# A convolution's setup rearranged: rounding of the angle tables moved from DVE to Pool, x loads between the tables, h copied in four parts, x's first stage woven into h's spectra

## Chip, cores, metric

One core of one Trainium2 chip. The metric is the device time of one execution in microseconds (us), median of the runs; lower is better. DVE is VectorE, ACT ScalarE, POOL GpSimd, PE TensorE, PEld its weight loads, SP SyncE. To evict is to copy a matmul's result out of the accumulators (PSUM) into SBUF. "Third stage" below is the first matmul of the convolution's third stage, the landmark by which the setup is measured: everything before it is setup, everything behind it the change doesn't touch.

## The reference

```python
Xf = np.fft.rfft(x, n=2*S, axis=1)            # x (8, 5696, 128), h (5696, 128)
Hf = np.fft.rfft(h, n=2*S, axis=0)
y  = np.fft.irfft(Xf * Hf[None], n=2*S, axis=1)[:, :S]
theta = y @ w_theta
yr = einsum('ts,bsd->btd', w_tok_r, y*cos(theta)); yi = einsum('ts,bsd->btd', w_tok_i, y*sin(theta))
u = y + yr + yi
out = u + maximum(u @ w_ch, 0)
```

## The kernel before

The convolution runs as four stages of matmuls with tables of sines: f1 (first stage), w (twiddles, second stage), r (third), e (fourth). The tables are computed on the chip: Pool makes angles, DVE reduces them to a fraction of a turn, ACT takes the sine. (Adding the constant MAGIC and taking it off again rounds to a whole number; a cosine needs the absolute value as well.) The spectra of h (its second-stage results) are made once and kept in memory; then come eight groups of x, and behind them the large matmuls that take most of the time. The order in which instructions stand in each engine's queue is made when the kernel is built, from the order in the code and estimated readiness; each engine then works its queue strictly in order.

```python
def turns_of(pattern, base, lanes, m, per, quarter=None):     # angle -> turns in [-0.5, 0.5]
    t, k = (two tiles of 11*NB floats, two buffers each)
    nc.gpsimd.iota(k, pattern=pattern, base=base, ...)
    nc.gpsimd.tensor_scalar(t, k, lanes, 1.0 / per, op0=mult, op1=mult)
    if quarter is not None: quarter(t)
    nc.vector.tensor_scalar(k, t, MAGIC, None, op0=add)                            # rounding
    nc.vector.scalar_tensor_tensor(t, k, MAGIC, t, op0=ALU.subtract, op1=ALU.subtract)
    return t, k

def absolute(k, r):
    nc.vector.scalar_tensor_tensor(k, r, -1.0, r, op0=mult, op1=ALU.max)

def w_table(k0):                                              # 15 of 90 columns: 960 elements
    t, k = turns_of([[1, 15], [N1, N2]], k0, lane[:, 0:1], P, NF)
    sine(w_t2[:, k0:k0 + 15, :N2], t3, 1)
    cosine(w_t2[:, k0:k0 + 15, N2:2 * N2], t3, k3)            # absolute, then ACT
    nc.vector.tensor_scalar(w_t2[..., 2 * N2:], w_t2[..., :N2], -1.0, None, op0=mult)

for k0 in (0, 15, 30):
    w_table(k0)
nc.vector.tensor_copy(h16[:NB], u_t[...])                     # h, one copy
x16s = {0: load_x(0)}                                         # 16 transfers of x
steps, a_h = stage_a(h16, True)                               # first stage of h, DVE and ACT evict
woven(steps, [w_table(45), w_table(60), w_table(75)])
for c in range(NCK):
    h_chunk(c)                                                # spectra of h
...
a0, load0, b0 = front(0)                                      # first stage of x, ACT alone evicts
woven(a0, [r_table(0, r_u), r_table(1, r_v), s_table] + load0)
woven(b0, [e_table(n0) for n0 in range(0, EN, 11)])           # second stage and products
```

## Time and profile before

| | before |
|---|---|
| median of 3 runs | 2176.91 us (2175.84 to 2178.12) |
| span of the profiled run | 2175.5 us |
| copy of h starts | 12.5 us |
| x's first stage is over (its second begins) | 63.6 us |
| third stage | 86.6 us |
| DVE busy up to it, idle | 67.3 us, 19.3 us |

The stretches, the timeline of the start and the groups that carry this are shown in the prediction. To read them: busy times of one engine may be added up, those of several may not, since engines work beside each other; an idle stretch of an engine counts only where that engine sets the end.

### The profile page before, as it was taken

Reading aid. Unit: us, or ns where it says so; the run is one execution under the profiler, and the core shown is the slowest. Engines: PE = TensorE matmul, PEld = TensorE weight load, DVE = VectorE, ACT = ScalarE, POOL = GpSimd, SP = SyncE. Lnnn points to the kernel's source line nnn. Section 1 sums busy time; section 2 is a strip of 40 time slices with the busy share of each in tenths; the row PEclk is TensorE's granted clock in tenths of the full one; section 3 lists DMA queues with packets and bytes.
Section 4 is the critical chain, followed back from the end, with each engine's and each line's share of the span. In section 5 each row is a group of like instructions: output and inputs, shape, how many; then the busy total and the mean of one; then the engine's idle time right before and its main releaser. Section 6 shows DMA issues by size and latency. Waiting matters only on the chain.

```text
span 2175.5 us, 41105 instructions
## 1 busy us (share of the span) xinstructions
PE 1998.2 (92%) x15545; PEld 1125.1 (52%) x15723; DVE 1619.4 (74%) x2920; ACT 670.6 (31%) x984; POOL 857.1 (39%) x1572
## 2 busy tenths in 40 slices
PE   4788898763899999999999999899999999999998
PEld 4787888652344444444444444344444444444444
DVE  7767767767778888888877667667777777776867
ACT  5877877574132333333210000001111111111111
POOL 5301010002344645445466544354545453535350
PEclk8788889987899999999999999999999999999999
DMA  7356463579988989899999869687878787879794
GB/s 146 89 125 163 128 162 118 172 185 275 236 156 175 182 169 168 167 179 176 176 169 162 138 115 291 106 133 137 148 132 152 132 151 130 152 131 153 126 158 91
DMA packets 409382, 340.38 MB, mean 156 GB/s; under 512 B 83303, under 2 KB 363751, under 8 KB 408071
## 3 DMA queue, kind: packets, MB, share of 16 engines
q0 software_dynamic: 221312, 143.00, 48.7%
q1 hardware_dynamic: 183552, 179.93, 28.5%
q10 hardware_dynamic: 4320, 14.81, 1.8%
q8 instruction: 123, 2.02, 0.4%
q14 instruction: 75, 0.61, 0.1%
HBM read 381.83 MB, written 97.93 MB: 221 GB/s over the span
## 4 chain that ended last, share of the span: by engine, by line
PE 65%; DMA 5%; DVE 4%; issue 2%; ACT 2%; POOL 1%; SPq 1%; DVEq 0%; ACTq 0%; POOLq 0%
PE m L910 59%; DMA b<-z_hbm 3%; PE m L878 2%; DMA z_hbm<-zz 2%; DVE c L917 1%; PE v L680 1%; PE utp L673 1%; PE m L914 1%; DVE wt L591 1%; PE m L833 1%; POOL wb L582 1%; PE m L831 1%; ACT mag L404 0%; ACT red L405 0%; PE theta_ps L382 0%
## 5 line engine op out<-in xcount | busy, mean ns | idle before, releaser
L582 POOL DMA_DIRECT2D wb<-in_moe_w_tok_i_dram x720 | 387.9, 547 | 679.3 <-DVE wt L591 602.6
L591 DVE STREAM_TRANSPOSE wt<-wb 128x384 f32<-128x384 f32 (+2 forms) x720 | 360.2, 524 | 117.1 <-PE m L910 71.2
L582 POOL DMA_DIRECT2D wb<-in_moe_w_tok_r_dram x720 | 386.6, 548 | 146.2 <-DVE wt L591 107.0
L910 PE MATMUL m<-b,wt 128*128 128x512 bf16 x1803 | 425.7, 381 | 7.1 <-DVE wt L591 2.4
L910 PEld LDWEIGHTS <-wt 128*128 128x128 bf16 x1848 | 181.3, 98 | 225.0 <-issue 5.7
L917 DVE TENSOR_TENSOR c<-c,m 128x512 f32<-128x512 f32 x420 | 271.0, 671 | 0.4 <-PE m L910 0.4
L675 ACT ACTIVATE uts<-utp 128x512 bf16<-128x512 bf16 (+1 forms) x90 | 53.2, 592 | 607.3 <-PE utp L673 607.3
L320 PE MATMUL ps<-r_u,u_t 128*128 128x128 f16 x1024 | 133.0, 228 | 14.9 <-DVE u_t L304 11.7
L321 PE MATMUL ps<-r_v,v_t 128*128 128x128 f16 x1024 | 131.7, 227 | 0.0
L670 ACT ACTIVATE ub<-c 128x512 bf16<-128x512 f32 (+1 forms) x90 | 56.3, 628 | 224.9 <-DVE c L846 139.7
L127 POOL DMA_DIRECT2D x<-in_x_dram x64 | 34.2, 541 | 201.3 <-PE ps L190 189.3
L320 PEld LDWEIGHTS <-u_t 128*128 128x128 f16 x1024 | 106.0, 103 | 13.6 <-DVE u_t L304 13.5
L321 PEld LDWEIGHTS <-v_t 128*128 128x128 f16 x1024 | 104.9, 103 | 5.2 <-issue 3.7
L304 DVE TENSOR_TENSOR u_t<-xs,hs 128x1024 f16<-128x1024 f16 x96 | 69.6, 725 | 41.9 <-ACT xs L302 31.5
L302 ACT ACTIVATE xs<-ps 128x1024 f16<-128x1024 f32 x96 | 95.3, 1017 | 17.6 <-DVE v_t L304 8.7
L878 PE MATMUL m<-b,wt 128*128 128x512 bf16 x344 | 79.3, 387 | 15.3 <-ACT red L405 14.5
L190 PE MATMUL ps<-f_t,x 89*128 89x180 f16 x512 | 84.5, 310 | 8.0 <-ACT xs L302 5.9
L208 PEld LDWEIGHTS <-w_t 64*128 64x128 f16 x3240 | 65.5, 106 | 38.1 <-issue 24.7
L580 POOL COPY wb<-b 128x2 bf16<-128x2 bf16 x4 | 0.5, 179 | 213.2 <-DMA z_hbm<-zz 213.2
L190 PEld LDWEIGHTS <-x 89*128 89x128 f16 x512 | 73.8, 237 | 10.1 <-issue 9.4
L384 ACT ACTIVATE red<-theta_ps,magic 128x512 f32<-128x512 f32 (+1 forms) x46 | 31.6, 687 | 140.8 <-PE theta_ps L382 107.4
L623 ACT ACTIVATE yb<-tpz 128x512 bf16<-128x512 bf16 (+1 forms) x46 | 27.4, 597 | 153.6 <-PE tpz L621 137.4
(2713 smaller groups left out, 3824.5 us busy)
## 6 DMA issues: line engine op xcount, KB each, us to landing
wb<-in_moe_w_tok_r_dram POOLq DMA_DIRECT2D x352, 96.0 KB, 4.5
wb<-in_moe_w_tok_i_dram POOLq DMA_DIRECT2D x352, 96.0 KB, 5.0
wb<-in_moe_w_tok_r_dram POOLq DMA_DIRECT2D x352, 80.0 KB, 4.2
wb<-in_moe_w_tok_i_dram POOLq DMA_DIRECT2D x352, 80.0 KB, 3.7
hs<-hf_hbm SPq DMA_DIRECT2D x192, 128.0 KB, 3.2
cp_hbm<-c SPq DMA_DIRECT2D x88, 256.0 KB, 2.3
c<-cp_hbm SPq DMA_DIRECT2D x88, 256.0 KB, 4.0
out_dram<-c SPq DMA_DIRECT2D x88, 256.0 KB, 4.2
```

Source lines behind the costliest of these rows:

```text
L190: nc.tensor.matmul(ps[:, i // 2, (i % 2) * 2 * K1:(i % 2 + 1) * 2 * K1], lhs(q + i), f1_t[:NB], start=True, stop=True)
L208: nc.tensor.matmul(ps[:, e, j * HD:(j + 1) * HD], w_t2[rows, c0 + j, N2 * (1 - ri):N2 * (3 - ri)], a_st["a"][rows, ri * K1 + c0 + j, :], s ...
L302: nc.scalar.activation(xs[:, :, :, :ck], ps, AF.Copy)
L304: nc.vector.tensor_tensor(uv[r][:, :, :, c0:c0 + ck], xs[:, :, :, :ck], hv[:, r:r + 1, :, :ck].to_broadcast([P, 2, HD, ck]), op=mult)
L320: nc.tensor.matmul(o, u_t[:, at:at + P], r_u, start=True, stop=False)
L321: nc.tensor.matmul(o, v_t[:, at:at + P], r_v, start=False, stop=True)
L582: nc.gpsimd.dma_start(wb[32 * i:32 * i + 32, :ng, :nj * 64], bass.AP(tensor=a.tensor, offset=a.offset + row0 * S + p * H + i * QR + j0 * 6 ...
L591: nc.vector.transpose(wt.rearrange("p j t r -> p (j t r)").bitcast(F32).rearrange("p (j g t) -> p g j t", j=TJ, g=4)[:, :ng, :nj], wb[:, : ...
L670: nc.scalar.activation(ub[:m].rearrange("p b d -> p (b d)"), c[:m], AF.Copy)
L878: nc.tensor.matmul(ms[n // 2 * 2 + h], a[n][:, j, :, r], bts[jj][n % 2 * 2 + h][:, r, :], start=(n % 2 == 0 and jj == 0 and r == 0), stop= ...
L910: nc.tensor.matmul(ms[q], a[q][:, j, :, r], bts[jj][q][:, r, :], start=(jj == 0 and r == 0), stop=(jj == NJ - 1 and r == 1 and q not in left))
L917: nc.vector.tensor_tensor(c, z, ms[q], op=op)
```

## The change

Intent: DVE, the fullest engine of the setup, should not stand behind the transfer of h, should have less to do per table, and x's first stage should not have to wait for h's last spectrum. The core of the diff:

```diff
+    def part(e, n0):  # one of eight x pieces
+                with tc.issue_after(rounded[-1]) if bp == 0 else ExitStack():
                     nc.gpsimd.dma_start(x16s[bp][...], ...)
 def turns_of(...)
-        nc.gpsimd.iota(k, pattern=pattern, base=base, ...)
-        nc.gpsimd.tensor_scalar(t, k, lanes, 1.0 / per, op0=mult, op1=mult)
+        nc.gpsimd.tensor_scalar(t, index_[:m], float(base), lanes[:m], op0=add, op1=mult)
-        nc.vector.tensor_scalar(k, t, MAGIC, None, op0=add)
+        rounded.append(nc.gpsimd.tensor_scalar(k, t, magic[:m], 1.0, op0=add, op1=mult).ins)
 def absolute(k, r)
-        nc.vector.scalar_tensor_tensor(k, r, -1.0, r, op0=mult, op1=ALU.max)
+        nc.vector.tensor_scalar(k.bitcast(I32), r.bitcast(I32), 0x7FFFFFFF, None, op0=ALU.bitwise_and)
 # w tables of 10 columns (640 elements) instead of 15, e tables of 7 rows instead of 11
-    for k0 in (0, 15, 30):
-        w_table(k0)
-    nc.vector.tensor_copy(h16[:NB], ...)
-    x16s = {0: load_x(0)}
+    x_steps = load_x(0)
+    last = w_table(0)
+    for n in range(2):
+        x_steps[n]()
+        w_table(TW + n * TW)
+    for d0 in range(0, HD, 16):
+        with tc.issue_after(last):
+            nc.vector.tensor_copy(h16[:, :, :, d0:d0 + 16], ...)
+    steps, a_h = stage_a(h16, True, s1)                 # a tile of its own
+    woven(steps, [f for n in range(3) for f in (x_steps[2 + n], w_steps[n])] + x_steps[5:])
...
+    steps, a_st = stage_a(x..., g == 0)                 # group 0: DVE evicts half
+    woven(([h_chunk(c) ...], 0.0, 0.6), (w_steps[3:], 0.0, 0.25), (a0, 0.5, 1.0), (load0, 0.6, 0.8),
+          (e_steps[:2] + [r tables, s_table], 0.4, 1.0))
+    woven(b0, (e_steps[2:], 0.0, 0.8))
```

(`woven` sorts steps by their place between the two given fractions; `issue_after` puts an instruction behind another in the order.)

More of the change, by code (lines that the diff above doesn't have):

```diff
@@ L13 @@
 F16 = mybir.dt.float16
+I32 = mybir.dt.int32
 add = mybir.AluOpType.add
@@ L114 @@
     uv = [t[:, :UVW].rearrange("p (e d k) -> p e d k", e=2, k=K1) for t in (u_t, v_t)]
-    h16 = s1.tile([P, 2, N2, HD], F16)
     for p0, p1 in ((0, 80), (80, NB)):
@@ L119 @@
                                     ap=[[N2 * D, p1 - p0], [1, N2 * D]]))
+    x16s = {}
     def load_x(bp):
-        x16 = fx.tile([P, 2, N2, D], F16, tag="x16", name="x16")
-        for e in range(2):
+        def part(e, n0):
+            if (e, n0) == (0, 0):
+                x16s[bp] = fx.tile([P, 2, N2, D], F16, tag="x16", name="x16")
             src = x[2 * bp + e]
-            for n0 in range(0, N2, 16):
-                for p0, p1 in ((0, 80), (80, NB)):
+            for p0, p1 in ((0, 80), (80, NB)):
+                with tc.issue_after(rounded[-1]) if bp == 0 else ExitStack():
                     nc.gpsimd.dma_start(
-                        x16[p0:p1, e, n0:n0 + 16, :].rearrange("p n d -> p (n d)"),
+                        x16s[bp][p0:p1, e, n0:n0 + 16, :].rearrange("p n d -> p (n d)"),
                         bass.AP(tensor=src.tensor, offset=src.offset + (p0 * N2 + n0) * D,
                                 ap=[[N2 * D, p1 - p0], [1, 16 * D]]))
-        return x16
-    lane = fc.tile([P, 2], F32)
+        return [lambda e=e, n0=n0: part(e, n0) for e in range(2) for n0 in range(0, N2, 16)]
+    lane = fc.tile([P, 5], F32)
     for p0 in (0, 64):
@@ L138, with index @@
                    allow_small_or_imprecise_dtypes=True)
-    def turns_of(pattern, base, lanes, m, per, quarter=None):
+    for c, (src, per) in enumerate(((1, N1), (0, NF), (1, NF)), 2):
+        nc.vector.tensor_scalar(lane[:, c:c + 1], lane[:, src:src + 1], 1.0 / per, None, op0=mult)
+    TW, TE = 10, 7
+    def index(pattern, pool, tag="index"):
         n = 1
@@ L144, in turns_of @@
             n *= c
-        t = s2.tile([P, 11 * NB], F32, tag="turn", name="turn")[:m, :n]
-        k = s2.tile([P, 11 * NB], F32, tag="whole", name="whole")[:m, :n]
-        nc.gpsimd.iota(k, pattern=pattern, base=base, channel_multiplier=0,
-                       allow_small_or_imprecise_dtypes=True)
-        nc.gpsimd.tensor_scalar(t, k, lanes, 1.0 / per, op0=mult, op1=mult)
+        k = pool.tile([P, n], F32, tag=tag, name="index")
+        nc.gpsimd.iota(k, pattern=pattern, base=0, channel_multiplier=0, allow_small_or_imprecise_dtypes=True)
+        return k
+    rounded = []
+    def turns_of(index_, base, lanes, m, quarter=None):
+        n = index_.shape[1]
+        room, small = (P, "_s") if n <= P else (TW * N2, "")
+        t = s2.tile([P, room], F32, tag="turn" + small, name="turn")[:m, :n]
+        k = s2.tile([P, room], F32, tag="whole" + small, name="whole")[:m, :n]
+        nc.gpsimd.tensor_scalar(t, index_[:m], float(base), lanes[:m], op0=add, op1=mult)
         if quarter is not None:
             quarter(t)
-        nc.vector.tensor_scalar(k, t, MAGIC, None, op0=add)
+        rounded.append(nc.gpsimd.tensor_scalar(k, t, magic[:m], 1.0, op0=add, op1=mult).ins)
         nc.vector.scalar_tensor_tensor(t, k, MAGIC, t, op0=ALU.subtract, op1=ALU.subtract)
@@ L166, with r_table, quarter, s_table @@
     f1_t = fc.tile([P, 2 * K1], F16)
-    t, k = turns_of([[1, K1]], 0, lane[:NB, 1:2], NB, N1)
+    t, k = turns_of(index([[1, K1]], s1, "f_index"), 0, lane[:, 2:3], NB)
     sine(f1_t[:NB, K1:], t, -1)
     cosine(f1_t[:NB, :K1], t, k)
+    r_u = fc.tile([P, P], F16)
+    r_v = fc.tile([P, P], F16)
+    sgn = fc.tile([P, N2], F32)
+    def r_table(n_, r_):
+        def quarter(t):
+            nc.vector.tensor_scalar(t, t, 1.0 / N2, None, op0=mult)
+            for q0 in range(2):
+                for q1 in range(2):
+                    a_ = t[64 * q0:64 * q0 + 64, 64 * q1:64 * q1 + 64]
+                    nc.vector.tensor_scalar(a_, a_, 0.25 * (1 + n_ + q0 - q1), None, op0=add)
+        t, k = turns_of(r_index, 0, lane[:, 0:1], P, quarter)
+        sine(k, t, 1)
+        nc.vector.tensor_scalar(r_[:, :N2 + EN], k[:, :N2 + EN], 0.125, None, op0=mult)
+        nc.vector.tensor_scalar(r_[:, N2 + EN:], k[:, N2 + EN:], -0.125, None, op0=mult)
+    def s_table():
+        t, k = turns_of(s_index, 0, lane[:, 1:2], P, lambda t: nc.vector.tensor_scalar(t, t, 0.5, None, op0=mult))
+        absolute(k, t)
+        nc.vector.tensor_scalar(k, k, -4.0, 1.0, op0=mult, op1=add)
+        nc.vector.memset(sgn, 1.0)
+        nc.vector.tensor_scalar(sgn[:, EN:], sgn[:, EN:], k, None, op0=mult)
     w_t2 = fc.tile([P, K1, 3 * N2], F16)
+    w_index = index([[1, TW], [N1, N2]], s1)
     def w_table(k0):
-        t, k = turns_of([[1, 15], [N1, N2]], k0, lane[:, 0:1], P, NF)
+        t, k = turns_of(w_index, k0, lane[:, 3:4], P)
         t3, k3 = (z.rearrange("p (k n) -> p k n", n=N2) for z in (t, k))
-        sine(w_t2[:, k0:k0 + 15, :N2], t3, 1)
-        cosine(w_t2[:, k0:k0 + 15, N2:2 * N2], t3, k3)
-        nc.vector.tensor_scalar(w_t2[:, k0:k0 + 15, 2 * N2:], w_t2[:, k0:k0 + 15, :N2],
-                                -1.0, None, op0=mult)
-    def stage_a(lhs, both=False):
+        sine(w_t2[:, k0:k0 + TW, :N2], t3, 1)
+        cosine(w_t2[:, k0:k0 + TW, N2:2 * N2], t3, k3)
+        return nc.vector.tensor_scalar(w_t2[:, k0:k0 + TW, 2 * N2:], w_t2[:, k0:k0 + TW, :N2],
+                                       -1.0, None, op0=mult).ins
+    def stage_a(lhs, both=False, home=None):
         st = {}
@@ L186, in chunk @@
             if q == 0:
-                st["a"] = fa.tile([P, 2 * K1, HD], F16, tag="a", name="a_")
+                st["a"] = (home or fa).tile([P, 2 * K1, HD], F16, tag="a", name="a_")
             ps = psum()
@@ L220, in woven @@
             f()
-    for k0 in (0, 15, 30):
-        w_table(k0)
-    nc.vector.tensor_copy(h16[:NB], u_t[:NB, :N2 * D].rearrange("p (n h d) -> p h n d", h=2, d=HD))
-    x16s = {0: load_x(0)}
-    steps, a_h = stage_a(lambda q: h16[:NB].rearrange("p h n d -> p (h n) d")[:, :, q], True)
-    woven(steps, [lambda k0=k0: w_table(k0) for k0 in range(45, K1, 15)])
+    x_steps = load_x(0)
[3 more added lines that the diff above has]
+        w_table(TW + n * TW)
+    h16 = fa.tile([P, 2 * K1, HD], F16, tag="a", name="h16").rearrange("p k d -> p (k d)")[:NB, :N2 * D].rearrange(
+        "p (h n d) -> p h n d", h=2, d=HD)
+    for d0 in range(0, HD, 16):
+        with tc.issue_after(last):
+            nc.vector.tensor_copy(h16[:, :, :, d0:d0 + 16], u_t[:NB, :N2 * D].rearrange(
+                "p (n h d) -> p h n d", h=2, d=HD)[:, :, :, d0:d0 + 16])
+    steps, a_h = stage_a(lambda q: h16.rearrange("p h n d -> p (h n) d")[:, :, q], True, s1)
+    w_steps = [lambda k0=k0: w_table(k0) for k0 in range(3 * TW, K1, TW)]
+    woven(steps, [f for n in range(3) for f in (x_steps[2 + n], w_steps[n])] + x_steps[5:])
     hst = [t[:, :6 * D * CK].rearrange("p (c h d k) -> p c h d k", c=6, h=2, k=CK) for t in (u_t, v_t)]
-    nc.gpsimd.memset(hst[(NCK - 1) // 6][:, (NCK - 1) % 6], 0.0)
+    with tc.issue_after(rounded[-1]):
+        nc.gpsimd.memset(hst[(NCK - 1) // 6][:, (NCK - 1) % 6], 0.0)
     def h_chunk(c):
@@ L247, in h_chunk @@
                 h_[64 * ri:64 * ri + 64].rearrange("p h d k -> p h (d k)"))
-    for c in range(NCK):
-        h_chunk(c)
-    nc.gpsimd.memset(u_t[:, UVW:], 0.0)
-    nc.gpsimd.memset(v_t[:, UVW:], 0.0)
-    r_u = fc.tile([P, P], F16)
-    r_v = fc.tile([P, P], F16)
-    e_t = fc.tile([P, EN, 2, NB], F16)
-    sgn = fc.tile([P, N2], F32)
-    def r_table(n_, r_):
-        def quarter(t):
-            for q0 in range(2):
-                for q1 in range(2):
-                    a_ = t[64 * q0:64 * q0 + 64, 64 * q1:64 * q1 + 64]
-                    nc.vector.tensor_scalar(a_, a_, 0.25 * (1 + n_ + q0 - q1), None, op0=add)
-        t, k = turns_of([[0, 2], [1, N2]], 0, lane[:, 0:1], P, N2, quarter)
-        sine(k, t, 1)
-        nc.vector.tensor_scalar(r_[:, :N2 + EN], k[:, :N2 + EN], 0.125, None, op0=mult)
-        nc.vector.tensor_scalar(r_[:, N2 + EN:], k[:, N2 + EN:], -0.125, None, op0=mult)
+    e_t = fc.tile([P, EN, 2, NB], F16)
     def e_table(n0):
-        t, k = turns_of([[1, 11], [N2, NB]], n0, lane[:K1, 1:2], K1, NF)
+        n = min(TE, EN - n0)
+        t, k = turns_of(e_index[:, :n * NB], n0, lane[:, 4:5], K1)
         t3, k3 = (z.rearrange("p (n m) -> p n m", m=NB) for z in (t, k))
-        sine(e_t[:K1, n0:n0 + 11, 1, :], t3, -1)
-        cosine(e_t[:K1, n0:n0 + 11, 0, :], t3, k3)
-    def s_table():
-        t, k = turns_of([[0, 1]], 1, lane[:, 1:2], P, 2)
-        absolute(k, t)
-        nc.vector.tensor_scalar(k, k, -4.0, 1.0, op0=mult, op1=add)
-        nc.vector.memset(sgn, 1.0)
-        nc.vector.tensor_scalar(sgn[:, EN:], sgn[:, EN:], k, None, op0=mult)
+        sine(e_t[:K1, n0:n0 + n, 1, :], t3, -1)
+        cosine(e_t[:K1, n0:n0 + n, 0, :], t3, k3)
     LEAD = 4
@@ L361, in front @@
         x16 = x16s[bp].rearrange("p b n d -> p (b n) d")
-        steps, a_st = stage_a(lambda q: x16[:NB, :, dh * HD + q])
+        steps, a_st = stage_a(lambda q: x16[:NB, :, dh * HD + q], g == 0)
         return (steps, *stage_b(a_st, dh))
     a0, load0, b0 = front(0)
-    woven(a0, [lambda: r_table(0, r_u), lambda: r_table(1, r_v), s_table] + load0)
-    woven(b0, [lambda n0=n0: e_table(n0) for n0 in range(0, EN, 11)])
+    with tc.issue_after(rounded[-1]):
+        nc.gpsimd.memset(u_t[:, UVW:], 0.0)
+        nc.gpsimd.memset(v_t[:, UVW:], 0.0)
+        e_index = index([[1, TE], [N2, NB]], s1, "e_index")
+        r_index, s_index = index([[0, 2], [1, N2]], s1, "r_index"), index([[0, 1]], s1, "s_index")
+        nc.vector.tensor_scalar(s_index, s_index, 1.0, None, op0=add)
+    e_steps = [lambda n0=n0: e_table(n0) for n0 in range(0, EN, TE)]
+    woven(([lambda c=c: h_chunk(c) for c in range(NCK)], 0.0, 0.6), (w_steps[3:], 0.0, 0.25), (a0, 0.5, 1.0),
+          (load0, 0.6, 0.8), (e_steps[:2] + [lambda: r_table(0, r_u), lambda: r_table(1, r_v), s_table], 0.4, 1.0))
+    woven(b0, (e_steps[2:], 0.0, 0.8))
     setup.close()
@@ L505, in next_x @@
             def next_x(bp=bp):
-                x16s[bp + 1] = load_x(bp + 1)
+                for part in load_x(bp + 1):
+                    part()
             a_ = a_ + [next_x]
```

## The prediction

> **What bounds the kernel now.** I read the page first, for where a change to the setup can count at all, then the table of stretches, then the timeline of the first 90 us, then the groups of instructions by shape, for prices.
>
> Page, busy time by engine, and the span in 40 slices of 54 us:
>
> ```profile
> PE 1998.2 (92%) x15545; PEld 1125.1 (52%) x15723; DVE 1619.4 (74%) x2920; ACT 670.6 (31%) x984; POOL 857.1 (39%) x1572
> ...
> PE   4788898763899999999999999899999999999998
> DVE  7767767767778888888877667667777777776867
> ```
>
> The kernel as a whole is bound by PE. Only the first slice and a bit is setup; there PE is at 4 tenths. From slice 12 on PE is full, doing work that the change doesn't touch. So the change can win or lose only in the setup, and what it wins there should reach the end as a shift of everything behind it.
>
> Stretches that I cut at the events named below (columns: stretch, its length, busy us of each engine with the number of instructions, granted clock, DMA share, GB/s):
>
> ```profile
> 0.00:12.50 12.50, 0.00 (x0) 0.00 (x0) 0.92 (x7) 1.94 (x3) 9.13 (x21) 1.00 0.81 146
> 12.50:30.70 18.20, 10.48 (x64) 9.52 (x65) 18.13 (x21) 11.80 (x14) 10.14 (x16) 1.00 0.52 85
> 30.70:50.50 19.80, 10.22 (x361) 9.59 (x360) 16.64 (x30) 11.90 (x13) 8.85 (x14) 0.72 0.78 191
> 50.50:63.60 13.10, 10.50 (x66) 9.80 (x65) 9.68 (x14) 12.68 (x18) 8.17 (x4) 0.50 0.49 114
> 63.60:86.60 23.00, 12.38 (x373) 10.93 (x373) 21.98 (x32) 20.12 (x21) 4.95 (x2) 0.57 0.36 107
> 86.60:130.00 43.40, 37.81 (x740) 36.20 (x741) 26.29 (x30) 29.20 (x37) 8.42 (x16) 0.81 0.60 132
> ```
>
> First stretch: h comes in. Second: first stage of h. Third: second stage of h (spectra to memory). Fourth: first stage of x, group 0. Fifth: its second stage with the products. At 86.6 the first matmul of the third stage starts, and behind it PE is busy 87%. In the setup DVE (third pair) is the fullest: 18.1 of 18.2, 16.6 of 19.8, 9.7 of 13.1, 22.0 of 23.0. In the fourth stretch ACT takes its place (12.7 of 13.1), since ACT alone evicts x's first stage. In the first, DVE does 0.9 us in 12.5: it has nothing to do.
>
> Why, in the timeline:
>
> ```profile
> 12.51 2.29 DVE L224 COPY h<-u_t 89x8192 f16<-89x8192 f16 x1 [6.69 <-DMA u_t<-in_h_dram]
> 14.72 0.65 DVE L152 TENSOR_SCALAR whole<-turn 128x960 f32<-128x960 f32 x1
> 14.85 5.47 PEld L190 LDWEIGHTS <-h 89*128 89x128 f16 x37 [14.85 <-DVE h L224]
> ...
> 20.11 0.99 POOL L147 IOTA whole<- 128x960 f32 x1 [9.47 <-ACT w_t L164]
> ...
> 30.72 4.42 PE L208 MATMUL ps<-a__163,w_t 64*128 64x64 f16 x159 [3.69 <-DVE a__163 L195]
> ```
>
> The copy of h stands on DVE's queue ahead of the rounding of the first two twiddle tables. Pool had prepared those by 6.8 and 10.0 us, but they wait behind a copy that waits for h (landed at about 12.5). So DVE idles 6.7 us, Pool's third table waits 9.5 us for a buffer, and PE starts at 14.85.
>
> The prices (groups of instructions by shape in the first 90 us; after the count, busy us and mean ns):
>
> ```profile
> L195 DVE CAST a__163<-ps 128x720 f16<-128x720 f32 x8 | 7.1, 898 | 0.0
> L160 DVE SCALAR_TENSOR_TENSOR whole<-turn 128x960 f32<-128x960 f32 x6 | 7.0, 1161 | 0.0
> L153 DVE SCALAR_TENSOR_TENSOR turn<-whole,turn 128x960 f32<-128x960 f32 x6 | 6.9, 1149 | 0.1
> L153 DVE SCALAR_TENSOR_TENSOR turn<-whole,turn 90x979 f32<-90x979 f32 x3 | 4.3, 1431 | 0.1
> L152 DVE TENSOR_SCALAR whole<-turn 128x960 f32<-128x960 f32 x6 | 3.9, 658 | 0.0
> L160 DVE SCALAR_TENSOR_TENSOR whole<-turn 90x979 f32<-90x979 f32 x3 | 3.8, 1270 | 0.1
> L152 DVE TENSOR_SCALAR whole<-turn 90x979 f32<-90x979 f32 x3 | 3.8, 1269 | 3.4 <-POOL turn L149 3.4
> L178 DVE TENSOR_SCALAR w_t<-w_t 128x960 f16<-128x960 f16 x6 | 2.5, 421 | 0.0
> ```
>
> **What the skill says.** (1) "VectorE: DVE Perf Modes", the perf-mode tier table: a tensor_scalar on fp32 in SBUF runs at 2x, a two-tensor operation on fp32 at 1x. The trace agrees: 658 ns against 1149 and 1161 for the same 960 elements. So turning the absolute value from a scalar_tensor_tensor into a tensor_scalar (a bitwise and on the same bits) should nearly halve it; that a bitwise operation gets the 2x rate no run has shown yet. (2) "Advanced Engine Details and Errata", VectorE Performance Modes, the note under the mode summary: the second Vector SBUF port is shared with GpSimd, so Pool and 2-port Vector instructions block each other. The trace fits: the three multiplies of Pool on 90x979 took 2.42, 1.40 and 3.85 us, and DVE's scaling of the second rotation table took 1.80 us (128x97) beside a 2.44 us iota, 0.21 us for the first. The change moves rounding from DVE to Pool, so this is its risk. (3) "TensorE: Matmul & The Clock Gate", Part 1: idleness throttles the array to half rate. Granted clock 0.50 to 0.72 from 30.7 to 86.6 fits; a denser setup may get a little of it back, which I don't count.
>
> **The change, part by part.** Slopes first. DVE tensor_scalar fp32: 658 ns at 960 elements, 204 at 90, so 0.52 ns per element: 491 at 640, 482 at 623, 389 at 445. Two-tensor: 1149 and 249, so 1.03 per element: 818, 801, 617. The negated copy, half the first slope: 338 at 640.
>
> - Twiddle tables: six of 960 cost DVE 658 + 1149 + 1161 + 421 = 3389 each, 20.3 us. Nine of 640 without the rounding (Pool's now) and with the cheap absolute value: 818 + 491 + 338 = 1647, 14.8 us. DVE: -5.5.
> - e tables: three cost 3.8 + 4.3 + 3.8 = 11.9. Five (four of 623, one of 445): 4 x 1283 + 1006 = 6.1. DVE: -5.8, of which some 2.9 is old contention (three undisturbed ones would be 3 x 3.0).
> - First stage of x, group 0: half of 16 evictions go from ACT to DVE at 898 ns. DVE: +7.2; ACT: -8 x 0.84 = -6.7.
> - h copy in four parts: each (2.29 - 0.15)/4 + 0.15 = 0.69, sum 2.7. DVE: +0.45, but PE can start after the first part.
> - Small tables: roundings leave (-1.0), scalings come (+0.8): nothing.
> - Pool: an iota and a multiply per table become an add-multiply and a rounding. A twiddle table was 1.01 + 1.19 = 2.2 us (x6 = 13.2); I take two passes of 0.8 (1.19 x 640/960), x9 = 14.4, plus index tables once. Pool is busy under half of most stretches, so this is beside the path unless it blocks DVE.
> - Order: the copy is held behind the first table, so DVE works while h is under way. x's pieces come one per table; before, four of them were issued between 5 and 10.1 us and shared the DMA engines with h. By 11.25 us some 1.66 MB had moved, while h needs 1.46; h alone could be in at 10 to 10.5 us.
> - Buffers: h's first-stage result moves into its own tile, so x's first stage no longer has to wait for h's last spectrum (before, strictly one after the other, 50.45).
>
> Sum on DVE up to the third stage: before 0.92 + 18.13 + 16.64 + 9.68 + 21.98 = 67.4 busy and 19.3 idle, together 86.6. After: 67.4 - 5.5 - 5.8 + 7.2 + 0.45 = 63.7 busy. Idle at the start: tables begin at about 7.5 us (Pool has f's and the first table's two passes to do), so 6.6; some 1 more until h lands; later stalls as before, 3.2 + 3.4 + 1.0 = 7.6, less perhaps 0.6 as stages overlap. Sum 63.7 + 6.6 + 1 + 7 = 78.3, so the third stage starts 8.3 us earlier.
>
> Check by stages: h's copy starts at 10.5 rather than 12.5, PE at about 11.2; h's first stage is over near 28 (was 30.7); spectra, last three tables and x's first stage hold some 27 us of DVE work and 24 us of PE work, done near 57 (was 63.6); the products, with three e tables and 16.5 us of multiplications, take 21 to 22 (was 23): third stage at 78 to 79. Same answer.
>
> 2176.9 - 8.3 = 2168.6; I say 2168.5.
>
> **The rivals.** (a) Pool and DVE block each other: nine tables have two Pool passes each next to 2x DVE operations. For: the stretched instructions above. Against: DVE's 2x work shrinks too. If each of the 28 new Pool passes cost DVE 0.2 us, 5.6 us are gone: 2174. (b) PE becomes the setup's bound in the middle: its 24 us at half clock are close to DVE's 27, and the in-order queues may interleave the stages badly, as the copy of h did. Gain 3 to 4: 2173. (c) Everything overlaps well, the contended 3 us on the rotation table vanish and idle falls to half: 13 to 15 us, 2162 to 2164. (d) The gain is swallowed behind the setup, say by a transfer. Against: in the stretch behind it PE is 87% busy and DMA at 0.60, so a shift should pass; then 2177.
>
> **Range and chances.** (a) and (b) pull up, (c) down, so 2161 to 2176. A 2% gain would be 43.5 us, half the setup: not reachable by these sums. Slower by 2% would need the setup half as long again. 0.98 for within 2%.
>
> **What would show it.** First instruction of h's copy near 10.5 us and DVE busy before it; absolute value near 0.5 us per 640; x's first stage overlapping h's spectra; first matmul of the third stage at 78 to 79; the rest shifted rigidly. It is wrong if bitwise operations run at 1x (0.8 us each, 3 us lost), if Pool's passes take over 1.2 us, or if the third stage starts early and the end does not follow.

## The result, and the profile after

Four runs: median 2179.24 us (2174.76 to 2180.97) against 2177.51 us of the kernel before. The ratio is 1.0006, 95% interval 0.9989 to 1.0023: the same. (A ratio is the mean time of one kernel's fast runs over that of the other's of the same rounds, so not quite the ratio of the medians.) The forecast was 2168.5, range 2161 to 2176.

The profiled run happened to be the fastest of the four (2174.76). The third stage started at 83.6 us instead of 86.6. Stretches of the changed kernel, cut at the same events as those of before, but for the last cut, which is 0.4 us behind the third stage (stretch, length, busy us of PE, PEld, DVE, ACT, POOL, granted clock, DMA share, GB/s):

```profile
0.00:12.50 12.50, 0.00 (x0) 0.00 (x0) 3.90 (x13) 3.68 (x5) 9.96 (x24) 1.00 0.79 145
12.50:26.60 14.10, 10.48 (x64) 9.43 (x64) 13.41 (x21) 10.49 (x14) 7.03 (x10) 1.00 0.49 78
26.60:52.80 26.20, 12.16 (x372) 11.01 (x373) 23.06 (x38) 16.63 (x20) 24.08 (x32) 0.63 0.80 182
52.80:62.70 9.90, 8.28 (x52) 7.68 (x51) 9.03 (x18) 8.22 (x11) 3.02 (x4) 0.50 0.42 99
62.70:84.00 21.30, 12.56 (x375) 11.24 (x375) 19.33 (x34) 17.73 (x21) 2.08 (x2) 0.58 0.42 119
```

The first stage of h is 4.1 us shorter (14.1 against 18.2) and the second stage of x about 2, but spectra and first stage of x together take 36.1 us (26.2 + 9.9) where they took 32.9 (19.8 + 13.1). In the third stretch Pool is busy 24.1 of 26.2 us, more than any other engine; before it was 8.9 of 19.8.

DVE's groups up to the third stage (busy us and mean ns behind the count):

```profile
L167 DVE SCALAR_TENSOR_TENSOR turn<-whole,turn 128x640 f32<-128x640 f32 x9 | 8.0, 896 | 3.9 <-POOL whole L166 3.9
L174 DVE TENSOR_SCALAR whole<-turn 128x640 int32<-128x640 int32 x9 | 6.3, 704 | 0.1
L167 DVE SCALAR_TENSOR_TENSOR turn<-whole,turn 90x623 f32<-90x623 f32 x4 | 4.0, 998 | 0.0
L217 DVE TENSOR_SCALAR w_t<-w_t 128x640 f16<-128x640 f16 x9 | 3.1, 345 | 0.7 <-ACT w_t L171 0.5
L195 DVE TENSOR_SCALAR turn<-turn 64x64 f32<-64x64 f32 x8 | 2.6, 388 | 0.1
L174 DVE TENSOR_SCALAR whole<-turn 90x623 int32<-90x623 int32 x4 | 2.5, 617 | 0.0
L167 DVE SCALAR_TENSOR_TENSOR turn<-whole,turn 128x128 f32<-128x128 f32 x2 | 1.5, 742 | 0.0
```

Every one but the negated copy (L217: 345 ns, 338 worked out) is longer than I had worked out (818 and 491 ns for the two groups of 640, 801 and 482 for the two of 623) or than before the change (185 for L195, the quarter additions, which add quarter turns in the rotation tables; 296 for the subtraction on 128x128). The timeline shows how; DVE and Pool at the start:

```profile
8.51 1.35 DVE L174 TENSOR_SCALAR whole<-turn 128x640 int32<-128x640 int32 x1
8.71 0.80 POOL L166 TENSOR_SCALAR whole<-turn,magic 128x640 f32<-128x640 f32 x1
10.62 0.79 POOL L163 TENSOR_SCALAR turn<-index,lane 128x640 f32<-128x640 f32 x1
12.49 1.90 DVE L270 COPY h<-u_t 89x2048 f16<-89x2048 f16 x3 [2.34 <-DMA u_t<-in_h_dram]
14.30 0.82 DVE L167 SCALAR_TENSOR_TENSOR turn<-whole,turn 128x640 f32<-128x640 f32 x1
15.64 0.48 DVE L174 TENSOR_SCALAR whole<-turn 128x640 int32<-128x640 int32 x1
```

The same absolute value takes 0.48 us with Pool idle (15.64) and 1.35 us when a Pool pass of 0.80 us begins inside it (8.51): nearly the two added up, while the Pool pass is as long as ever. Elsewhere it is Pool that waits: its pass on 90x623 took 2.22 us at 46.93 beside DVE's table steps, and 0.79 us at 50.19. A subtraction has two inputs in SBUF; "GPSIMD Engine Reference", Specifications, names such DVE instructions beside those in a 2-port mode as the ones that conflict with Pool. The runs agree: the two subtractions on 128x128 took 742 ns on average here, and 279 ns in e9 below, where Pool had one pass less. The lines also show that h's copy still starts at 12.5, and that the second table's first DVE step (14.30), whose rounding Pool had done by 9.5, still stands behind that copy while DVE idles 2.3 us. During the spectra, Pool's order looks as if it mattered too:

```profile
29.01 3.33 POOL L130 DMA_DIRECT2D x<-in_x_dram  x6
33.53 1.19 POOL L152 IOTA index<- 128x623 f32 x3
34.83 1.70 POOL L163 TENSOR_SCALAR turn<-index,lane 128x640 f32<-128x640 f32 x2
41.12 2.31 PE L247 MATMUL ps<-a__160,w_t 64*128 64x64 f16 x80 [5.96 <-ACT w_t L178]
```

Six x issues and three index tables stand ahead of the passes for the last twiddle tables, and PE then waits 6.0 us for a table.

### The profile page after: what moved, and what is told of

Read it like the earlier page. It is cut to its first block, busy times and chain, and to the rows that moved or that the text cites. A ratio compares the mean times of both kernels' runs of the same rounds, so it can differ in the third digit from the quotient of the medians.

```text
span 2172.9 us, 41172 instructions
## 1 busy us (share of the span) xinstructions
PE 1994.7 (92%) x15545; PEld 1121.2 (52%) x15723; DVE 1618.9 (75%) x2938; ACT 667.1 (31%) x986; POOL 861.5 (40%) x1587
## 4 chain that ended last, share of the span: by engine, by line
PE 64%; DMA 6%; DVE 5%; issue 2%; POOL 1%; ACT 1%; SPq 0%; DVEq 0%; ACTq 0%; POOLq 0%
PE m L941 57%; DMA b<-z_hbm 2%; DMA z_hbm<-zz 2%; PE m L909 2%; DVE c L948 2%; DVE wt L622 1%; PE v L711 1%; PE utp L704 1%; POOL wb L613 1%; PE m L945 1%; DMA wb<-in_moe_w_tok_i_dram 1%; PE m L864 1%; PE m L862 1%; PE theta_ps L412 0%; PE tpz L652 0%
## 5 line engine op out<-in xcount | busy, mean ns | idle before, releaser
L706 ACT ACTIVATE uts<-utp 128x512 bf16<-128x512 bf16 (+1 forms) x90 | 53.2, 592 | 607.2 <-PE utp L704 607.2
L342 PEld LDWEIGHTS <-u_t 128*128 128x128 f16 x1024 | 106.3, 104 | 12.6 <-DVE u_t L326 12.5
L229 PEld LDWEIGHTS <-x 89*128 89x128 f16 x512 | 73.8, 237 | 13.2 <-issue 12.8
```

Source lines behind the costliest of these rows:

```text
L229: nc.tensor.matmul(ps[:, i // 2, (i % 2) * 2 * K1:(i % 2 + 1) * 2 * K1], lhs(q + i), f1_t[:NB], start=True, stop=True)
L342: nc.tensor.matmul(o, u_t[:, at:at + P], r_u, start=True, stop=False)
```

## The experiments

Sixteen further runs. Those of no rounds were looked at once, with a trace: their total says little, since it scatters by more than the effects sought, but their setup repeats. The two kernels run more than once show that: third stage at 86.6 and 87.0 us before, at 83.6, 82.6 and 82.8 us after. So a difference of about 1 us in the third stage says nothing.

| kernel | third stage | DVE busy up to it | idle (difference) |
|---|---|---|---|
| before, again | 86.6, 87.0 | 67.3, 67.4 | 19.3, 19.6 |
| predicted | 78.3 | 63.7 | 14.6 |
| changed, again, third | 83.6, 82.6, 82.8 | 68.3, 68.3, 68.5 | 15.3, 14.3, 14.3 |
| e1_tables_first | 84.1 | 68.4 | 15.7 |
| e2_h_alone | 83.6 | 68.1 | 15.5 |
| e3_round_dve | 82.4 | 71.3 | 11.1 |
| e4_abs_two_tensor | 85.5 | 73.1 | 12.4 |
| e6b | 85.5 | 69.1 | 16.4 |
| e7_act_evicts | 85.6 | 63.0 | 22.6 |
| e8_before_copy_held | 85.1 | 69.8 | 15.3 |
| e9_round_act | 80.9 | 66.0 | 14.9 |
| e5_copy_later, again | 80.3, 80.6 | 69.4 (first) | 10.9 |
| e10_dve_copy_later | 80.2 | 71.6 | 8.6 |
| e11_act_copy_later | 79.9 | 66.9 | 13.0 |
| e12_pool_twice | 91.2 | 74.8 | 16.4 |

All outputs are right. Theory C, formed from the trace above: Pool's passes stretch DVE's instructions, and what the arithmetic of the tables saves goes there. Rivals: P (order on PE or Pool keeps stages apart), D (DVE's own work), and a gain given back behind the setup.

**Is the total settled?** `before_again` is the unchanged kernel, `after_again` and `after_third` are the changed one, no edit.

> The kernel before against itself. Theory (the gain is real but smaller than forecast: the third stage started at 83.6 us instead of 86.6 in the traces, 3.0 us, and the rest scatters): ratio 1.000, its runs within about 3 us of each other, third stage again at 86 to 87 us. Rival (chance in the later transfers decides the total): its runs spread over 5 us or more, or the ratio lies outside 0.999 to 1.001.

> The changed kernel as it is, for a better interval. Theory that a shift of the setup reaches the end: third stage at 83 to 84 us again and the total 2 to 4 us below the kernel before, ratio 0.998 to 0.999. Rival that the gain is given back behind the setup: third stage at 83 to 84 us, ratio 1.000 or more, and a later landmark of the trace (last matmul of the third stage, first of the big matmuls, last matmul) no longer shifted.

> The changed kernel once more, to settle its total: two sets so far gave 1.0006 and 0.9983. Theory (3.0 to 4.4 us pass to the end): ratio 0.998 to 0.999. Rival (nothing reaches the end): 1.000 or more.

Measured: before_again 2178.24 us, ratio 1.000 (0.9987 to 1.0013), but its six runs spread over 6.3 us (2175.27 to 2181.59), so the rival's mark for the spread is met as well. after_again 2173.26 us, 0.9983 (0.9969 to 0.9997); after_third 2178.05 us, 0.9992 (0.9972 to 1.0012). With the first set that is 1.0006, 0.9983 and 0.9992: the interval excludes 1 in one set of three, and no set is clear of its rival. Their mean, 0.9994, would be 1.4 us; a setup gain of 3.0 to 4.4 us lies inside the scatter. The traces say more than the totals. From the third stage to the last of the large matmuls the two traces of before took 2073.8 and 2075.0 us, the three of the changed kernel 2074.2, 2070.7 and 2078.1; over all 18 traces, with setups from 79.9 to 91.2 us, it is 2074.5 on average, standard deviation 2.3, 2070.1 to 2078.9, with a correlation of 0.03 to the time of the third stage. The rest of the kernel takes the same whatever the setup did, but it scatters by more than the change wins.

**e1_tables_first: the order on Pool.**

```diff
-    woven(steps, [f for n in range(3) for f in (x_steps[2 + n], w_steps[n])] + x_steps[5:])
+    woven(steps, [f for n in range(6) for f in (x_steps[2 + n], w_steps[n])])
-    woven((h chunks, 0.0, 0.6), (w_steps[3:], 0.0, 0.25), (a0, 0.5, 1.0), ...)
+    woven((h chunks, 0.0, 0.6), (a0, 0.5, 1.0), ...)
```

> The last three twiddle tables are given out with the first stage of h, one x load between each, instead of after all x loads, the memsets and the index tables. Theory (Pool's order keeps the last tables back: in the trace six x issues, three memsets and three iotas, 29.0 to 34.8 us, stand before them, and the small tables before the very last; PE waits 6 and 3.5 us for them): PE's waits for twiddle tables in the spectra fall from 9.5 us to under 4, the last spectrum of h is done at 45 to 47 us instead of 51, the third stage starts 3 to 6 us earlier (78 to 81 us), total down by the same. Rival (the middle is bound by the work of DVE as such, 23 of 26 us): third stage within 1 us of 83.6.

Measured: last spectrum at 48.9 instead of 50.8, PE still waits 8.2 us for tables, third stage 84.1; 2175.15 us, ratio 0.998 (0.9966 to 0.9995). The third stage is where the rival put it, and the lower total is within the scatter of the sets. The order on Pool is not what holds the setup; this theory fell. After the spectra DVE was busy 13.2 of 14.6 us, with the small tables that had moved in between x's evictions.

**e2_h_alone: does x delay h?**

```diff
     for n in range(2):
-        x_steps[n]()
         w_table(TW + n * TW)
-    woven(steps, [... (x_steps[2 + n], w_steps[n])] + x_steps[5:])
+    woven(steps, [... (x_steps[n], w_steps[n])] + x_steps[3:])
```

> No x load is given out before h is copied. Theory of my prediction (x pieces share the DMA engines with h and delay it): h lands at 10 to 10.5 us, its copy starts there instead of 12.49. Rival (the x pieces come behind h in the same queue and cost it nothing; h takes until 12.5 by itself): copy starts at 12.3 to 12.6 us as in both kernels. Nothing is expected of the total, which one run can't settle.

```profile
12.37 0.69 DVE L269 COPY h<-u_t 89x2048 f16<-89x2048 f16 x1 [1.42 <-DMA u_t<-in_h_dram]
```

With no x issue in front of it, the copy starts at 12.37 us: h, alone on the queue, is ready no earlier. The 2 us that I gave to this step were not there. The same trace shows where they are: all 1.46 MB of h had moved by 10.0 us, as I had estimated, and no packet follows after 10.9, yet DVE was released 2.4 us after the last bytes. What lies between these two no run here shows.

**e3_round_dve: the rounding back on DVE.**

```diff
-        nc.gpsimd.tensor_scalar(t, index_[:m], float(base), lanes[:m], op0=add, op1=mult)
+        rounded.append(nc.gpsimd.tensor_scalar(t, index_[:m], float(base), lanes[:m], op0=add, op1=mult).ins)
-        rounded.append(nc.gpsimd.tensor_scalar(k, t, magic[:m], 1.0, op0=add, op1=mult).ins)
+        nc.vector.tensor_scalar(k, t, MAGIC, None, op0=add)
```

> The rounding goes back from Pool to DVE, all else as in the changed kernel. Theory C (Pool and DVE hold each other up): in the changed kernel some DVE groups are longer than without neighbours (absolute value of 640: 704 ns mean against 480 undisturbed; quarter additions 388 against 185; in all about 7 us up to the third stage). If that is what ate the gain, this kernel's groups fall back to 480 to 520 and 185 to 220 ns, which pays for the 7 us of rounding that DVE gets back (9 x 0.49 + 4 x 0.48 + 0.9): third stage at 82 to 85 us, as in the changed kernel (82.6 to 83.6). Rival (moving the rounding was a plain gain for DVE): groups as long as before, third stage at 88 us or later.

Third stage at 82.4, as in the changed kernel. DVE's rounding groups add up to 8.8 us (5.0 + 1.9 + 0.8 + 0.6 + 0.4 + 0.1), yet DVE's busy time is only 3.0 us above the changed kernel's. So 5.8 us of DVE time that the changed kernel spends on other instructions are gone when Pool has one pass less. The groups of this kernel:

```profile
L174 DVE TENSOR_SCALAR whole<-turn 128x640 int32<-128x640 int32 x9 | 5.6, 625 | 0.1
L195 DVE TENSOR_SCALAR turn<-turn 64x64 f32<-64x64 f32 x8 | 1.9, 292 | 0.0
L167 DVE SCALAR_TENSOR_TENSOR turn<-whole,turn 128x128 f32<-128x128 f32 x2 | 0.8, 410 | 0.0
```

704, 388 and 742 ns have become 625, 292 and 410. They don't fall to the 480 and 185 that I expected; Pool's other pass is still there, which may be why. Moving the rounding to Pool was worth nothing that the third stage shows.

**e9_round_act: the rounding on ACT**, so that neither DVE nor Pool has it. As e3, but with

```diff
+        nc.scalar.activation(k, t, AF.Identity, bias=magic[:m])
```

> The rounding goes to ACT, all else as changed: DVE has no more work than in the changed kernel, Pool one pass less per table, ACT 9 x 0.83 + 5 x 0.8 + 1.5 = 13 us more (56 of 83 us busy so far). Theory C (Pool's passes stretch DVE's instructions): the absolute values of 640 fall from 704 to 600 or less, DVE's busy time up to the third stage from 68.5 to 65 or less, third stage at 79 to 82 us. Rival (ACT, which also stands in every table's chain, takes the place): third stage at 83 us or later though DVE's groups are shorter.

```profile
L167 DVE SCALAR_TENSOR_TENSOR turn<-whole,turn 128x640 f32<-128x640 f32 x9 | 7.3, 818 | 2.1 <-ACT whole L166 2.0
L174 DVE TENSOR_SCALAR whole<-turn 128x640 int32<-128x640 int32 x9 | 5.6, 620 | 0.1
L217 DVE TENSOR_SCALAR w_t<-w_t 128x640 f16<-128x640 f16 x9 | 3.9, 431 | 1.2 <-ACT w_t L171 1.2
```

Third stage at 80.9, 1.7 to 2.7 us earlier, with DVE's busy time at 66.0: 2.3 below the changed kernel. Right in direction, but less than the 3.5 expected; the absolute value missed its 600 too, and the negated copy grew.

**e12_pool_twice: the suspected cost made larger.** One line more in each table, the same rounding a second time on Pool.

> Pool rounds twice into the same tile (same values), so its passes per table are three instead of two; DVE's and ACT's work is as in the changed kernel. Theory C (Pool's passes stretch DVE's instructions and hold back the tables): absolute values of 640 at 750 ns or more (704), DVE's busy time up to the third stage 70 us or more (68.5), third stage at 86 us or later. Rival (Pool's passes lie beside DVE's work at no cost): DVE's groups as before, third stage at 82.5 to 84.

```profile
0.00:91.20 91.20, 43.90 (x861) 39.65 (x862) 74.79 (x120) 56.53 (x70) 63.72 (x89) 0.70 0.55 124
```

Third stage at 91.2, and DVE, with the same 120 instructions, busy 74.8 us instead of 68.3. The absolute values of 640 did not grow (670 against the 750 expected); the quarter additions (546 ns from 388), the subtraction of 640 (942 from 896) and, most of all, the one subtraction of the first table (2.41 us from 0.25) did. So the cost lands on different instructions in each kernel, and the sum shows it. The third stage came about 8 us later, of which 6.5 is DVE's busy time. The run can't say how much of the rest is Pool's own time in the chain of the tables: Pool was busy 63.7 us here, 46.2 in the changed kernel and 30.0 in e9.

**e4_abs_two_tensor: the absolute value in its old form.**

```diff
-        nc.vector.tensor_scalar(k.bitcast(I32), r.bitcast(I32), 0x7FFFFFFF, None, op0=ALU.bitwise_and)
+        nc.vector.scalar_tensor_tensor(k, r, -1.0, r, op0=mult, op1=ALU.max)
```

> The absolute value goes back to the two-tensor form, all else as in the changed kernel. Theory (the bitwise form saves DVE time, also where Pool is beside it): per 640 elements 818 to 900 ns instead of 704 mean, so 15 instructions cost 2 to 4 us more and the third stage comes 1 to 3 us later than 83. Rival (the cheap form is held up by Pool and saves nothing): third stage at 82 to 84 us.

Third stage at 85.5, and 1022 ns instead of 704 per 640 elements: the bitwise form is worth 2 to 3 us. The two-tensor form, too, is longer than the 818 to 900 expected.

**e7_act_evicts: x's first stage evicted by ACT alone** (`stage_a(..., g == 0)` without its last argument).

> ACT alone evicts x's first stage, as before the change; all else as changed. Theory D (DVE bounds the stretch): DVE is relieved of 8 x 0.90 = 7.2 us, ACT gets 8 x 0.8; x's first stage ends 2 to 4 us earlier than 62.7. Rival (the split of the evictions was right, ACT would bound it with 16 x 0.84 = 13.4 us as before the change): x's first stage ends at 64 us or later.

x's first stage ends at 65.8 and the third stage comes at 85.6, although DVE has 5.3 us less to do. Rival D fell: the split evictions are a gain of 2 to 3 us, even though they load the fullest engine. (DVE's idle time grew to 22.6 us: less work on DVE is a gain only if nothing else then sets the end.)

**e6b: x's first stage woven in earlier** (`(a0, 0.25, 1.0)` for `(a0, 0.5, 1.0)`).

> x's first stage is woven between h's spectra from a quarter of the way on (0.25 to 1.0) instead of from the half (0.5 to 1.0): in the built program 28 of its 64 matmuls stand before the last spectrum of h, instead of 8. Theory P (PE's order keeps the two stages one after the other, PE waits 6 and 3.5 us in the spectra and could do x there, 0.76 to 0.9 us a chunk): x's first stage ends 3 to 5 us earlier than 62.7 and the third stage starts at 78 to 81 us. Rival D (DVE's work bounds the stretch from 26.6 to 62.7, 32 us of 36): x's first stage ends at 61.5 to 63.5, third stage at 82 to 84.

Worse: the last spectrum at 53.2, x's first stage over at 64.8, third stage 85.5. From the table of waits (us in total, times, longest):

```profile
PEld L229 <- DMA x<-in_x_dram: 7.3, 1, 7.3
```

And from the timeline of PE (start us, us, engine, line, operation, out<-in, and in brackets the idle time before it with its releaser):

```profile
39.55 0.87 PE L229 MATMUL ps<-f_t,x 89*128 89x180 f16 x4 [7.15 <-DVE turn L167]
```

The weight load of the first x matmul waited 7.3 us, by the table for x to land. The matmul behind it names DVE's subtraction in a table (L167) instead, which ended in the same moment, so the profile does not quite settle which of the two came last; I read it as x. A spectrum behind that matmul in PE's queue cannot overtake it. Neither theory had this; it shows only that an earlier window than the given one doesn't help with these loads.

**e8_before_copy_held: one part alone**, on the kernel before: the copy of h in four parts, each put by `issue_after` behind the first twiddle table, and nothing else.

> The kernel before with one part of the change alone: h copied in four parts, held behind the first twiddle table. Theory (the order of DVE's queue at the start is a large part of what the change wins): DVE works some 3.4 us before h lands, PE starts at 13.2 instead of 14.8, and the third stage comes at 84 to 86 us instead of 86.6 to 87.0. Rival (the time won at the start is lost again in the spectra, which wait for the last tables): third stage at 86 to 87.5.

Third stage at 85.1: the order at the start alone is worth 1.5 to 1.9 us.

**e5_copy_later and e5_again: h's copy behind the second table.**

```diff
-    last = w_table(0)
+    w_table(0)
     for n in range(2):
         x_steps[n]()
-        w_table(TW + n * TW)
+        z = w_table(TW + n * TW)
+        last = last if n else z
```

> h's copy is held behind the second twiddle table instead of the first. Theory (DVE idles 2.3 us at 10.2 to 12.5 while the second table stands ready behind the copy): those 1.6 us of work are done before h lands, and the third stage comes 1 to 2 us earlier, 81 to 82. Rival (what bounds the middle is not touched): third stage at 82.6 to 83.6.

> The changed kernel with h's copy behind the second table, timed. Theory (the setup's gain passes to the end one to one): third stage at 80 to 81 us, 6 to 7 us below the kernel before, ratio 0.997. Rival (only part of it passes): ratio 0.9985 or more.

```profile
10.05 0.81 DVE L167 SCALAR_TENSOR_TENSOR turn<-whole,turn 128x640 f32<-128x640 f32 x1
10.90 0.98 DVE L174 TENSOR_SCALAR whole<-turn 128x640 int32<-128x640 int32 x1
12.38 2.76 DVE L271 COPY h<-u_t 89x2048 f16<-89x2048 f16 x3 [0.28 <-DMA u_t<-in_h_dram]
```

DVE now does the second table where it idled: 0.28 us of idle time before the copy instead of 2.34. Third stage at 80.3 and 80.6, 2.0 to 3.3 us earlier than in the changed kernel, slightly more than expected; timed, 2171.63 us, ratio 0.9969 (0.9952 to 0.9986), by the ratio 6.7 us below the kernel before (5.6 by the medians), as the theory that the gain passes to the end had it; the rival's 0.9985 lies at the very edge of the interval.

**e10_dve_copy_later and e11_act_copy_later: both edits**, e3 with e5 and e9 with e5.

> Rounding on DVE and h's copy behind the second table. With the rounding on DVE alone the third stage came at 82.4. Theory (the idle time before h lands takes one table's 2.1 us): 80 to 81.5 us. Rival: 82 to 83.

> Rounding on ACT and h's copy behind the second table, the two edits that brought the third stage to 80.9 and 80.3 us. Theory (they act on different things, blocking by Pool and idle time before h lands): third stage at 78 to 79.5 us, total 7 to 9 us below the kernel before, ratio 0.996 to 0.997. Rival (both shorten the same stretch, the chain of the tables then binds): third stage at 80 to 81, ratio 0.997 to 0.998.

e10: 80.2. e11: 79.9, hardly before e5's 80.3, so the two edits add up only in small part, against the 78 to 79.5 expected. ACT, now busy 68.9 of 79.9 us, stands in every table's chain, which may be why; no run tests it. Timed, e11 has a median of 2171.19 us, ratio 0.9961 (0.9944 to 0.9979): the lowest measured, below both kernels, though still within 2%, and its interval overlaps e5's.

## Why the prediction was wrong

- **What bounds, and where it can count: held.** All differences lie in the setup, and the stretch behind it was the same in 18 traces to within its scatter (standard deviation 2.3 us). The forecast of "within 2%" was right; the size was not.
- **The step that failed: "After: 67.4 - 5.5 - 5.8 + 7.2 + 0.45 = 63.7 busy".** DVE was busy 68.3 us in the profiled run and 68.3 and 68.5 in two more. The prices assumed that DVE's instructions take as long as alone. The twiddle tables cost 8.0 + 6.3 + 3.1 = 17.4 us, not 14.8; the e tables (with the one of 445 elements) 7.5, not 6.1: 4.0 of the 4.6 missing. Behind it stands the sentence on Pool, "this is beside the path unless it blocks DVE". It blocks, and Pool was the fullest engine of the third stretch (24.1 of 26.2 us). One Pool pass per table less gave DVE 5.8 us (e3) or 2.3 us (e9), one more took 6.5 us (e12). Why the three sizes differ is not shown; the order of the instructions differs too. That Pool's passes cost DVE time of this order is shown.
- **Why the prices were too low.** Counted by element, Pool made as many passes over the tables before the change: an iota and a multiply then, an add-multiply and a rounding now (2 x 5760 elements for the twiddles in both). But in the trace of before its twiddle passes lay mostly beside DVE's evictions or its idle time (20.1 to 23.0, 29.6 to 34.2, 40.2 to 42.6 us), so the twiddle prices read there were those of DVE nearly alone.
- **The sum "busy + idle" is no model of its own.** It always gives the right total afterwards, but idle time does not stay when busy time changes: over these runs it goes from 8.6 us (e10) to 22.6 (e7), and e7 had the predicted 63 us of busy time with the third stage at 85.6. For the changed kernel the idle time came out near the forecast, so the shortfall of 5.3 us (83.6 against 78.3) is 4.6 of busy and 0.7 of idle time.
- **The idle term was right in sum, 14.6 against 14.3 to 15.3, partly by luck, for its parts were not.** h was not ready at 10 to 10.5 us but at 12.4, and e2 shows that x was never the reason: half of what I wanted from the start was not to be had. The other half, DVE working before h lands, was got only for one table out of two, because the second again stood behind the copy; e5 shows 2.0 to 3.3 us in that.
- **The check by stages gave the same answer because it had the same fault.** h's first stage was over at 26.6 (I had said near 28). Spectra and x's first stage, put at 29 us, took 36.1. Two sums from one set of prices don't check each other.
- **The parts that held:** the cheap absolute value (0.48 us per 640 where Pool is idle, e4), the split evictions (+7.1 us on DVE as priced, and still a gain, e7), the second stage of x (20.9 us from 62.7 to the third stage, 21 to 22 forecast). "Small tables: nothing" held by luck: the scalings of the rotation tables fell from 3.8 to 0.8 us (the 3 us of rival (c)), while the quarter additions and the subtractions on 128x128 rose by 2.3.
- **Rival (a) was the right one, and its size came close:** it said 5.6 us gone and 2174. Its 0.2 us per pass was an assumption; 4.6 us over its 28 passes would be 0.16. The third stage moved by 3.0 to 4.4 us where 8.3 were forecast, which leaves 3.9 to 5.3 gone. I had its evidence in hand (the 1.80 us scaling beside a 2.44 us iota) and even counted 2.9 us of the old e tables as contention that would vanish, while putting Pool's passes beside DVE's.
- **Rival (b), PE at half clock, and point (3) on the clock:** the granted clock did not matter here. From 26.6 to 62.7 us it was 0.50 to 0.76 in two traces of the changed kernel and 1.00 in after_again; the matmuls of x's first stage took 356 ns in the median in either case, and the third stage came at 83.6, 82.8 and 82.6. That the in-order queues interleave the stages badly was tested by e1 and e6b, and neither order was better.
- **Open:** how much of the 3.0 to 4.4 us reaches the end in the changed kernel, and how much of what Pool's passes cost the third stage goes through DVE's longer instructions rather than through Pool's own time in the tables' chain. The traces show nothing that gives it back; the three timed sets (1.0006, 0.9983, 0.9992) can't confirm it.

## What to carry to other kernels

Work moved from a full engine to an idle one is free only if the two don't hold each other up, as DVE and Pool did here: price it from a stretch where both were busy, or subtract what the neighbour's passes cost. Look at which instruction stands next in a queue when its data is late: letting one more ready table pass ahead of h's copy won 2.0 to 3.3 us of setup, where the whole change had won 3.0 to 4.4. And where the rest of a kernel scatters by 2 us and more, judge a gain of 3 us by a landmark in the trace and not by the total.

## What the Trainium skill lacked or had wrong

- "VectorE: DVE Perf Modes", the perf-mode tier table, names no bitwise operation. A bitwise and on 640 int32 elements took 0.48 us, what the arithmetic tensor_scalar was priced at (0.49).
